# Gated MLP with channels on partitions: u and spatial products swapped, no transposes of the gated values

## The chip, the cores and the metric

The kernel runs on one core of a Trainium2 chip. The metric is the device time of one execution in microseconds. All inputs and the output lie in HBM in float32; the matmuls are in bfloat16.

## The reference

A sparse attention feeds a gated MLP. Shapes: batch 4, 8 heads, sequence 768, head size 64, so a token has 512 channels; the MLP widens them to 1024.

```python
scores = where(mask, q @ k.T / sqrt(64), -1e9)      # mask: band, edges and sampled blocks of 32
x = (softmax(scores) @ v), heads side by side       # 4 x 768 x 512
h = maximum(x @ w_in, 0.0)                          # 4 x 768 x 1024
u, v = h[..., :512], h[..., 512:]
v_n = (v - mean(v, -1)) / sqrt(var(v, -1) + 1e-6)
v_s = einsum('ts,bsd->btd', w_spatial, v_n) + b_spatial[None, :, None]
out = (u * v_s) @ w_out                             # 4 x 768 x 512
```

So the spatial product mixes tokens, its bias belongs to a token and is the same for all channels, and the output product mixes channels.

## The kernel before

The attention works on pairs of heads, 16 in all. A slot is one step of the main loop: a piece of the scores of one head (L408 for the first batch, L421 after it), the exponentials of it on ScalarE (L413, L424), and the product with the values of an earlier piece (L451, L469). VectorE divides by the row sums (L433, L434: rc, xn). Pairs after the first four get k and q transposed by a DMA (tr_dma, L367: nat to tt) and copied into kq by VectorE (split, L210: kq<-tt), five and three slots before their scores start. xn is transposed into xt, with channels on partitions and tokens along the row, by TensorE or by a DMA (L510, L501).

The MLP of a batch is dealt into the slots of the next one. Its 768 tokens are six chunks of 128; chunk c holds the tokens 6p + c. All its steps stand in a queue: for each of the six chunks a v product and a u product of NDM = 4 matmuls, then six spatial products of NCH = 6, then six output products of NDH = 4. A step is one matmul of 512 columns; run_queue takes some from the queue in each slot, about 2.25 on average, at a pace set by the number of steps left. What a step records is written out by hand in this order; each engine executes its own instructions strictly in the order recorded, and so does SP with its DMA requests. The MLP of the last batch has no slots left, and its steps run one behind another (the tail): last_x, then last_steps, then rest_steps.

Each product writes one PSUM bank (moe_ps: two banks in turn, six in the tail) and its last step records the eviction:

- v (L583, L184): relu into vn, chunk by chunk with tokens on partitions, then statistics (L588, L589) on VectorE; GpSimd makes the reciprocal deviation rstd for a group of chunks (L592, L594), and vn_one normalises a chunk in place (L184) at the earliest VN_AGE = 9 steps after its group; what is left is normalised ahead of the first spatial step.
- u: relu into un, on VectorE for batch 0 (L184), on ScalarE for the others (L617).
- spatial: one VectorE instruction adds the bias of the token (b_col, one value per partition and chunk) and multiplies by un in place (L623). Then a DMA on SP transposes two chunks of the gated values (un) into gt, with channels on partitions (L635). In the tail the sixth chunk is transposed by TensorE (g_transpose) and copied by VectorE.
- output: lhsT is gt, rhs w_out; the copy osb goes out by a DMA on SP, the very last half on ScalarE's queue (L661).

The spatial weights are loaded (ws_load), cast on GpSimd (ws_cast, L528) and transposed by DMA into w_spt in three pieces (ws_tr, L531). b_col is loaded by SP behind the first loads (L322). The order of SP's requests around slot 46 to 52 is: the transposition of pair 6 (tt), then the loads of k, q and v of a later pair, then the last piece of w_spt.

In the last batch the sequence of products is

```python
seq = m.in_steps("v0 v1 u0 v2 v3 v4 v5 u1 u2 u3 u4 u5", 3)
```

The first three steps of its first three products are recorded ahead of the transposition of the last xt, and their fourth steps behind it. xt of the last pair is copied in two parts, chunks 0 and 1 and chunks 2 to 5.

Of the kernel before, what the change touches and what calls it, by code (L numbers as in the profile page):

```python
# [10 lines left out]
FP32 = mybir.dt.float32  # L11
BF16 = mybir.dt.bfloat16
I32 = mybir.dt.int32
AF = mybir.ActivationFunctionType
ALU = mybir.AluOpType
# [11 lines left out]
def kernel(  # L27
# [16 lines left out]
    nc = tc.nc  # L44

    B, H, S, D = q.shape
# [3 lines left out]
    NCH = S // 128  # L50
# [25 lines left out]
    w_in_t = const.tile([128, NDM, DFF], BF16)  # L76
    w_out_t = const.tile([128, NDH, DM], BF16)
    w_spt = const.tile([128, NCH, NCH, 128], BF16)
    b_col = const.tile([128, NCH], FP32)
    mhalf = const.tile([128, NCH], FP32)  # L80

    kq = const.tile([128, H, 2 * S], BF16, name="kq")
# [99 lines left out]
    def ts(out, in0, s1, o0, s2=None, o1=None):  # L182
        kw = {} if o1 is None else {"op1": o1}
        nc.vector.tensor_scalar(out=out, in0=in0, scalar1=s1, scalar2=s2, op0=o0, **kw)  # L184
# [24 lines left out]
    def dve_copy(o, i):  # L209
        nc.vector.tensor_copy(out=o, in_=i)  # L210
# [47 lines left out]
    def bank(nm="ps", tag=None):  # L258
        return psum.tile([128, 1024], BF16, tag=tag or moe_tag(), bufs=2 if tag else 1, name=nm)

    def tr(ps, c, in_):
        nc.tensor.transpose(out=ps[:, c * 128:(c + 1) * 128], in_=in_, identity=ident)  # L262
# [53 lines left out]
    for i, x in enumerate(ORDER):  # L316
# [2 lines left out]
            rows(slice(2, 4), qcols(1), PL)  # L319
        for y in ORDER[i + AHEAD:i + AHEAD + 1]:  # L320
            ahead(y)
    nc.sync.dma_start(out=b_col, in_=moe_b_spatial.rearrange("(p c) -> p c", c=NCH))  # L322

    def second():
        ps2 = bank("ps2", "av")
# [191 lines left out]
    def ws_load(i):  # L517
        ws["f", i] = work.tile([128, S], FP32, tag="ws_f", bufs=6, name="ws_f")
        nc.sync.dma_start(out=ws["f", i],
                          in_=moe_w_spatial.rearrange("(p c) s -> c p s", c=NCH)[i])  # L520

    def ws_cast(i):
        if i % 2 == 0:
            ws["b", i // 2] = work.tile([128, 2, NCH, 128], BF16, tag="ws_b", bufs=2, name="ws_b")
        src = ws.pop(("f", i)).rearrange("p (s c) -> p c s", c=NCH)
        for c0 in range(0, NCH, NCH // 3):
            cs = slice(c0, c0 + NCH // 3)
            nc.gpsimd.tensor_copy(out=ws["b", i // 2][:, i % 2, cs], in_=src[:, cs])  # L528
# [9 lines left out]
    def moe_ps(last):  # L538
        if not last:
            return psum.tile([128, 512], FP32, tag=moe_tag(), bufs=1, name="ps_moe")  # L540
        tail_tags.rotate(1)
        if tail_tags[0] == "sc":
            return psum.tile([128, 1024], FP32, tag="sc", bufs=2, name="ps_sc")[:, 0:512]
        if tail_tags[0] == "moe":
            return psum.tile([128, 512], FP32, tag=moe_tag(), bufs=1, name="ps_t")
        return psum.tile([128, 512], FP32, tag="av", bufs=2, name="ps_t")

    def product(n, lhs, rhs, last, done, w=512):
        ref = {}
        out = []  # L550
        for i in range(n):
            def run(i=i):
                if i == 0:
                    ref["ps"] = moe_ps(last)
                nc.tensor.matmul(out=ref["ps"][:, 0:w], lhsT=lhs(i), rhs=rhs(i),  # L555
                                 start=(i == 0), stop=(i == n - 1))
                if i == n - 1:
                    done(ref["ps"][:, 0:w])
            out.append(run)
        return out  # L560
# [4 lines left out]
    class Moe:  # L565
        def __init__(self, b):
            self.b, self.last = b, b == B - 1
            w = lambda nm: work.tile([128, NCH, DH], BF16, tag=nm, bufs=1, name=nm)
            self.un, self.vn = w("un"), w("vn")
            self.gt = work.tile([128, NCH, NDH, 128], BF16, tag="gt", bufs=1, name="gt")  # L570
            self.mv = work.tile([128, NCH, 2], FP32, tag="mv", bufs=2)
            self.std = work.tile([128, NCH], FP32, tag="std", bufs=2)
            self.rstd = work.tile([128, NCH], FP32, tag="rstd", bufs=2)
            self.vn_due = deque()
            self.steps = 0
# [33 lines left out]
                ts(self.vn[:, tcc, :], self.vn[:, tcc, :], self.mv[:, tcc, 0:1], ALU.subtract,  # L609
                   self.rstd[:, tcc:tcc + 1], ALU.mult)  # L610

        def u_product(self, tcc):
            def done(ps):
                if self.b == 0 and tcc in U_DVE:
                    ts(self.un[:, tcc, :], ps, 0.0, ALU.max)
                else:
                    nc.scalar.activation(out=self.un[:, tcc, :], in_=ps, func=AF.Relu)  # L617
            return product(NDM, lambda g: self.xt(g, tcc), lambda g: w_in_t[:, g, 0:DH],
                           self.last, done)

        def s_product(self, tcc):
            def done(ps):
                nc.vector.scalar_tensor_tensor(out=self.un[:, tcc, :], in0=ps,  # L623
                                               scalar=b_col[:, tcc:tcc + 1],
                                               in1=self.un[:, tcc, :], op0=ALU.add,
                                               op1=ALU.mult)
                if self.last and tcc == NCH - 1:
                    return
                if self.last and tcc == NCH - 2:
                    g0 = tcc  # L630
                elif tcc % 2 == 1:
                    g0 = tcc - 1
                else:
                    return
                nc.sync.dma_start_transpose(  # L635
                    out=self.gt[:, g0:tcc + 1].rearrange("p t c n -> p (t c) n"),
                    in_=self.un[:, g0:tcc + 1, :].rearrange("p t d -> p (t d)"))
            return product(NCH, lambda s: w_spt[:, tcc, s, :], lambda s: self.vn[:, s, :],
                           self.last, done)


        def g_transpose(self):
            ps = bank("ps_g", "av")
            for d in range(NDH):
                tr(ps, d, self.un[:, NCH - 1, d * 128:(d + 1) * 128])
            dve_copy(self.gt[:, NCH - 1].rearrange("p c n -> p (c n)"), ps[:, 0:NDH * 128])

        def o_product(self, tcc, n):
            steps = []
            osb = {}  # L650
            parts = 2 if self.last and n == NCH - 1 else 1
            w = DM // parts
            for i in range(parts):
                cs = slice(i * w, (i + 1) * w)

                def done(ps, i=i, cs=cs):
                    if i == 0:
                        osb["t"] = work.tile([128, DM], FP32, tag="osb", bufs=6, name="osb")
                    on_act = self.b > 0 and (n + i) % 2 == 0
                    (act_copy if on_act else dve_copy)(osb["t"][:, cs], ps)  # L660
                    (nc.scalar if i else nc.sync).dma_start(  # L661
                        out=out[self.b].rearrange("(p c) d -> c p d", c=NCH)[tcc][:, cs],
                        in_=osb["t"][:, cs])
                steps += product(NDH, lambda d: self.gt[:, tcc, d, :],
                                 lambda d, cs=cs: w_out_t[:, d, cs], self.last, done, w)
            return steps

# [6 lines left out]
        def rest_steps(self):  # L674
            out = []
            for tcc in range(NCH):
                out += self.s_product(tcc)
            first = out[0]
            out[0] = lambda: ([self.vn_one(True) for _ in range(NCH)], first())
            for n, tcc in enumerate((0, 1, 5, 2, 3, 4) if self.last else range(NCH)):  # L680
                out += self.o_product(tcc, n)
                if self.last and n == 1:
                    out.insert(len(out) - 3, self.g_transpose)
            return out

    queue = deque()
# [20 lines left out]
    def when(slot, *fns):  # L707
        at.setdefault(slot, []).extend(fns)

    def c(f, *a, **kw):  # L710
        return lambda: f(*a, **kw)
# [57 lines left out]
    def last_x():  # L769
        moe_begin(B - 1)  # L770
        m = moe[B - 1]
        while queue:
            queue.popleft()()
        seq = m.in_steps("v0 v1 u0 v2 v3 v4 v5 u1 u2 u3 u4 u5", 3)
        n = NG - 1
        for i in (0, 1):
            for f in seq[i * NG:i * NG + n]:
                f()
        ps, xn = bank(), xn_ref.pop(("p", NP - 1))
        moe_tags.rotate(1)  # L780
        for cc in range(NCH):
            tr(ps, cc, pair_of(xn, cc))
        xt = xt_tile(NP - 1)
        for cs in (slice(0, TW), slice(TW, S)):
            dve_copy(xt[:, cs], ps[:, cs])
        for f in seq[2 * NG:2 * NG + n]:
            f()
        for i in (0, 1, 2):
            seq[i * NG + n]()
        last_steps.extend(seq[3 * NG:])  # L790
# [24 lines left out]
        when(ca, c(ws_cast, i))  # L815
    for i, sl in enumerate((24, 30, 50)):
        when(sl, c(ws_tr, i))
    when(50, *[c(w_out_load, g) for g in range(NDH)])
    when(58, *[c(w_out_cast, g, PL) for g in range(NDH)])

# [59 lines left out]
```

## Time and profile before

| what | value |
|---|---|
| median of 3 runs | 210.97 us (210.81 to 211.08) |
| the profiled execution: time, span of its instructions | 211.73 us, 209.9 us |
| TensorE busy | 201.3 us (96%) |
| weight loads busy (beside the matmuls) | 129.1 us (61%) |
| VectorE busy | 136.4 us (65%) |
| ScalarE busy | 168.8 us (80%) |
| GpSimd busy | 83.3 us (40%) |
| granted TensorE clock, mean | 0.996 |
| spatial eviction L623, 128x512 | 0.75 us each, 24 of them |
| last matmul starts, tail's spatial products start | 206.0 us, 192.9 us |

An engine's busy time is the union of its instructions. PE is TensorE's matmuls, PEld its weight loads, DVE is VectorE, ACT ScalarE, POOL GpSimd, SPq the queue of SP's requests. A timeline line gives the start, the time from the first start to the last end, engine, line and operation, out<-in, shapes and count; in brackets the idle time before it and who ended it. Matmuls overlap: the recorded time of one is longer than the distance to the next, so the pace is read from starts.

### The profile page before, as it was taken

Reading aid. Unit: us, or ns where it says so; the run is one execution under the profiler, and the core shown is the slowest. Engines: PE = TensorE matmul, PEld = TensorE weight load, DVE = VectorE, ACT = ScalarE, POOL = GpSimd, SP = SyncE. Lnnn points to the kernel's source line nnn. Section 1 sums busy time; section 2 is a strip of 40 time slices with the busy share of each in tenths; the row PEclk is TensorE's granted clock in tenths of the full one; section 3 lists DMA queues with packets and bytes.
Section 4 is the critical chain, followed back from the end, with each engine's and each line's share of the span. In section 5 each row is a group of like instructions: output and inputs, shape, how many; then the busy total and the mean of one; then the engine's idle time right before and its main releaser. Section 6 shows DMA issues by size and latency. Waiting matters only on the chain.

```text
span 209.9 us, 5319 instructions
## 1 busy us (share of the span) xinstructions
PE 201.3 (96%) x2106; PEld 129.1 (61%) x2140; DVE 136.4 (65%) x301; ACT 168.8 (80%) x222; POOL 83.3 (40%) x184
## 2 busy tenths in 40 slices
PE   8789999999999999999999999999999999999993
PEld 6569878766666666665566556665566556544441
DVE  7768987999874756484975454284985443476551
ACT  6979999999999999979998888979889787266021
POOL 6689869957828726006159051006220000012000
PEclk9999999999999999999999999999999999999998
DMA  5999799999999999999965497478501225610256
GB/s 162 330 357 344 222 314 285 251 301 359 250 338 188 264 165 296 270 219 345 210 216 112 116 247 179 153 177 262 102 3 35 53 53 116 222 54 0 50 146 228
DMA packets 64684, 41.96 MB, mean 200 GB/s; under 512 B 45716, under 2 KB 59412, under 8 KB 64660
## 3 DMA queue, kind: packets, MB, share of 16 engines
q1 hardware_dynamic: 64228, 41.24, 76.0%
q10 hardware_dynamic: 432, 0.39, 0.6%
q8 instruction: 16, 0.26, 0.5%
q14 instruction: 8, 0.07, 0.1%
HBM read 24.38 MB, written 6.29 MB: 146 GB/s over the span
## 4 chain that ended last, share of the span: by engine, by line
PE 87%; DMA 4%; DVE 2%; SPq 1%; ACT 1%; issue 1%; POOL 0%; ACTq 0%
PE ps_moe L555 31%; PE ps L421 22%; PE ps_av L469 13%; PE ps_t L555 7%; PE ps L408 6%; PE ps_av L451 4%; DMA st_k<-in_k_dram 4%; PE ps_sc L555 3%; PE ps L262 1%; SPq L108 1%; DVE kq L210 1%; ACT a_all L413 1%; DMA out_dram<-osb 1%; PE ps_av L262 1%; ACT osb L213 0%
## 5 line engine op out<-in xcount | busy, mean ns | idle before, releaser
L424 ACT ACTIVATE a_all<-ps 128x768 bf16<-128x768 f32 x144 | 113.7, 811 | 15.5 <-PE ps L421 7.2
L421 PE MATMUL ps<-kq 128*128 128x512 bf16 (+1 forms) x288 | 70.3, 325 | 0.2
L469 PEld LDWEIGHTS <-a_all 128*128 128x128 bf16 x864 | 46.6, 98 | 19.4
L469 PE MATMUL ps_av<-vv,a_all 128*128 128x65 bf16 x864 | 51.0, 194 | 0.1
L421 PEld LDWEIGHTS <-kq 128*128 128x128 bf16 x288 | 27.8, 97 | 30.1 <-issue 0.2
L555 PE MATMUL ps_moe<-w_in_t,xt 128*128 128x512 bf16 x128 | 39.4, 378 | 0.5
L413 ACT ACTIVATE a_all<-ps 128x1024 bf16<-128x1024 f32 x35 | 33.9, 1024 | 1.9 <-PE ps L408 1.4
L136 POOL CAST nat<-st_k 128x256 bf16<-128x256 f32 (+3 forms) x37 | 16.7, 482 | 42.9 <-DMA st_k<-in_k_dram 31.4
L555 PE MATMUL ps_moe<-vn,w_spt 128*128 128x512 bf16 x98 | 30.5, 378 | 0.6
L592 POOL TENSOR_SCALAR std<-mv 128x3 f32<-128x3 f32 (+1 forms) x9 | 2.1, 238 | 50.8 <-DVE mv L589 36.9
L408 PE MATMUL ps<-kq 88*128 88x256 bf16 (+1 forms) x136 | 21.0, 275 | 1.0 <-DVE kq L210 0.6
L623 DVE SCALAR_TENSOR_TENSOR un<-ps_moe,b_col,un 128x512 bf16<-128x512 f32 x18 | 13.5, 748 | 12.9 <-PE ps_moe L555 10.9
L555 PE MATMUL ps_moe<-w_out_t,gt 128*128 128x512 bf16 x66 | 20.2, 378 | 0.1
L555 PEld LDWEIGHTS <-xt 128*128 128x128 bf16 x192 | 15.2, 97 | 7.1 <-DVE xt L210 0.2
L433 DVE RECIPROCAL rc<-ps_av 128x6 f32<-128x6 f32 (+1 forms) x36 | 6.6, 184 | 19.9 <-PE ps_av L469 18.8
L434 DVE TENSOR_TENSOR xn<-ps_av,rc 128x384 bf16<-128x384 f32 (+1 forms) x36 | 18.5, 513 | 1.2
L136 POOL CAST nat<-st_q 128x256 bf16<-128x256 f32 (+2 forms) x41 | 17.2, 447 | 3.9 <-DMA st_q<-in_q_dram 3.6
L136 POOL CAST vv<-st_v 128x256 bf16<-128x256 f32 (+1 forms) x36 | 17.4, 516 | 3.1 <-DMA st_v<-in_v_dram 3.0
L588 DVE BATCH_NORM_STATS2 stats<-vn 128x6 f32<-128x512 bf16 x24 | 16.5, 688 | 1.5 <-ACT vn L583 0.9
L184 DVE TENSOR_SCALAR vn<-ps_moe 128x512 bf16<-128x512 f32 x18 | 12.3, 683 | 6.0 <-PE ps_moe L555 6.0
L451 PE MATMUL ps_av<-vv,a_all 128*128 128x65 bf16 x288 | 14.6, 194 | 1.0 <-POOL vv L136 1.0
L451 PEld LDWEIGHTS <-a_all 128*128 128x128 bf16 x288 | 13.5, 98 | 2.7 <-issue 1.5
(92 smaller groups left out, 215.5 us busy)
## 6 DMA issues: line engine op xcount, KB each, us to landing
st_v<-in_v_dram SPq DMA_DIRECT2D x16, 384.0 KB, 6.0
out_dram<-osb SPq DMA_DIRECT2D x23, 256.0 KB, 2.4
st_k<-in_k_dram SPq DMA_DIRECT2D x15, 384.0 KB, 4.4
st_q<-in_q_dram SPq DMA_DIRECT2D x12, 384.0 KB, 4.9
ws_f<-in_moe_w_spatial_dram SPq DMA_DIRECT2D x6, 384.0 KB, 4.7
w_f<-in_moe_w_in_dram SPq DMA_DIRECT2D x8, 256.0 KB, 5.6
w_f<-in_moe_w_out_dram SPq DMA_DIRECT2D x4, 256.0 KB, 5.6
st_q<-in_q_dram SPq DMA_DIRECT2D x3, 256.0 KB, 6.9
```

Source lines behind the costliest of these rows:

```text
L136: eng.tensor_copy(out=dst, in_=src)
L184: nc.vector.tensor_scalar(out=out, in0=in0, scalar1=s1, scalar2=s2, op0=o0, **kw)
L408: nc.tensor.matmul(out=ps[:, at:at + n * TW], lhsT=kq[0:KR, h, ci * 128:(ci + 1) * 128], rhs=kq[0:KR, h, qcols(t0, n)], start=True, stop=True)
L413: nc.scalar.activation(out=out, in_=ps, func=AF.Exp, scale=0.125)
L421: nc.tensor.matmul(out=ps[:, n0:n1], lhsT=kq[:, j % H, ci * 128:(ci + 1) * 128], rhs=kq[:, j % H, S + n0:S + n1], start=True, stop=True)
L424: nc.scalar.activation(out=a_ref["h", j][:, ci, :], in_=ps[:, 0:S], func=AF.Exp, scale=0.125)
L434: nc.vector.tensor_tensor(out=out, in0=ps[:, :, 0:D], in1=rc[:, 0:n].to_broadcast([128, n, D]), op=ALU.mult)
L451: nc.tensor.matmul(out=av_ref[u][:, to, :], lhsT=a_ref[u][:, at:at + 128], rhs=vv[pp % NVV][:, h, ci, :], start=(ci == 0), stop=(ci == NCH ...
L469: nc.tensor.matmul(out=av_ref[j][:, qc, :], lhsT=a_ref["h", j][:, ci, qc * 128:(qc + 1) * 128], rhs=vv[p % NVV][:, h, ci, :], start=(ci == ...
L555: nc.tensor.matmul(out=ref["ps"][:, 0:w], lhsT=lhs(i), rhs=rhs(i), start=(i == 0), stop=(i == n - 1))
L588: nc.vector.bn_stats(out=stats, in_=self.vn[:, tcc, :])
L623: nc.vector.scalar_tensor_tensor(out=self.un[:, tcc, :], in0=ps, scalar=b_col[:, tcc:tcc + 1], in1=self.un[:, tcc, :], op0=ALU.add, op1=AL ...
```

## The change

The u product takes w_in as the stationary operand and xt as the moving one, so u comes out with channels on partitions and tokens along the row. The spatial product takes the normalised v as the stationary operand and w_spt as the moving one, with the same result layout. un then has the layout that the output product needs, gt and its transposes go, and the output product reads un.

An area of a product is nd blocks of 128 channels by n chunks of 128 tokens, with nd x n = 4, so that it fills a bank and a step still streams 512 columns: one matmul of 512 where nd is 1, two of 256 where nd is 2. For u, batch 0 has six areas of two blocks by two chunks; the others two of these and four of one block by chunks 2 to 5. The spatial products have four areas of one block by chunks 0 to 3 and two of two blocks by chunks 4 and 5.

The bias now lies along the row and is the same on all partitions: SP loads the 768 values to all 128 partitions (b_load, slot 46), and VectorE copies them into the order of the chunks (b_row, slot 52). The eviction is two VectorE instructions: the add of b_row from PSUM into sb (float32), and the product with un in place.

In the last batch v2 is moved ahead of u0 and the output chunks come in the order 0 to 5.

```diff
-    b_col = const.tile([128, NCH], FP32)
+    b_row = const.tile([128, S], FP32)
...
-    nc.sync.dma_start(out=b_col, in_=moe_b_spatial.rearrange("(p c) -> p c", c=NCH))
...
+    def b_load():
+        ws["b_nat"] = work.tile([128, S], FP32, tag="ws_f", bufs=6, name="b_nat")
+        nc.sync.dma_start(out=ws["b_nat"], in_=moe_b_spatial.partition_broadcast(128))
...
-            self.un, self.vn = w("un"), w("vn")
-            self.gt = work.tile([128, NCH, NDH, 128], BF16, tag="gt", bufs=1, name="gt")
+            self.vn = w("vn")
+            self.un = work.tile([128, NDH, S], BF16, tag="un", bufs=1, name="un")
...
+        def in_place(self, d0, nd, c0, n):
+            return self.un[:, d0:d0 + nd, c0 * 128:(c0 + n) * 128]
+
+        def by_columns(self, k, d0, nd, c0, n, lhs, rhs, done):
+            ref, out = {}, []
+            mms = [(x, i) for x in range(nd) for i in range(k)]
+
+            def run(j):
+                if j == 0:
+                    ref["ps"] = moe_ps(self.last)
+                for x, i in mms[j * nd:(j + 1) * nd]:
+                    o = ref["ps"][:, x * n * 128:(x + 1) * n * 128]
+                    nc.tensor.matmul(out=o.rearrange("p (c t) -> p c t", c=n),
+                                     lhsT=lhs(i)[:, (d0 + x) * 128:(d0 + x + 1) * 128],
+                                     rhs=rhs(i), start=(i == 0), stop=(i == k - 1))
+                if j == k - 1:
+                    done(ref["ps"][:, 0:512].rearrange("p (d t) -> p d t", d=nd))
+            return [lambda j=j: run(j) for j in range(k)]
+
+        def u_product(self, i):
+            if self.b == 0:
+                area = (2 * (i % 2), 2, TC * (i // 2), TC)
+            else:
+                area = (2 * i, 2, 0, 2) if i < 2 else (i - 2, 1, 2, NCH - 2)
+            d0, nd, c0, n = area
...
-        def s_product(self, tcc):
+            return self.by_columns(
+                NDM, *area, lambda g: w_in_t[:, g, 0:DH],
+                lambda g: xt_ref[self.b * NG + g][:, c0 * 128:(c0 + n) * 128].rearrange(
+                    "p (c t) -> p c t", c=n), done)
+
+        def s_product(self, i):
+            area = (i, 1, 0, NCH - 2) if i < NDH else (2 * (i - NDH), 2, NCH - 2, 2)
+            d0, nd, c0, n = area
+
             def done(ps):
-                nc.vector.scalar_tensor_tensor(out=self.un[:, tcc, :], in0=ps,
-                                               scalar=b_col[:, tcc:tcc + 1],
-                                               in1=self.un[:, tcc, :], op0=ALU.add,
-                                               op1=ALU.mult)
...
-                nc.sync.dma_start_transpose(
-                    out=self.gt[:, g0:tcc + 1].rearrange("p t c n -> p (t c) n"),
-                    in_=self.un[:, g0:tcc + 1, :].rearrange("p t d -> p (t d)"))
-            return product(NCH, lambda s: w_spt[:, tcc, s, :], lambda s: self.vn[:, s, :],
-                           self.last, done)
-
-
-        def g_transpose(self):
-            ps = bank("ps_g", "av")
...
+                sb = work.tile([128, 512], FP32, tag="sb", bufs=2, name="sb").rearrange(
+                    "p (d t) -> p d t", d=nd)
+                nc.vector.tensor_tensor(
+                    out=sb, in0=ps, op=ALU.add,
+                    in1=b_row[:, None, c0 * 128:(c0 + n) * 128].to_broadcast([128, nd, n * 128]))
+                nc.vector.tensor_tensor(out=self.in_place(*area), in0=sb,
+                                        in1=self.in_place(*area), op=ALU.mult)
+            return self.by_columns(NCH, *area, lambda s: self.vn[:, s, :],
+                                   lambda s: w_spt[:, c0:c0 + n, s, :], done)
...
-                steps += product(NDH, lambda d: self.gt[:, tcc, d, :],
+                steps += product(NDH, lambda d: self.un[:, d, tcc * 128:(tcc + 1) * 128],
                                  lambda d, cs=cs: w_out_t[:, d, cs], self.last, done, w)
...
-            for n, tcc in enumerate((0, 1, 5, 2, 3, 4) if self.last else range(NCH)):
-                out += self.o_product(tcc, n)
-                if self.last and n == 1:
-                    out.insert(len(out) - 3, self.g_transpose)
+            for n in range(NCH):
+                out += self.o_product(n, n)
...
-        seq = m.in_steps("v0 v1 u0 v2 v3 v4 v5 u1 u2 u3 u4 u5", 3)
+        seq = m.in_steps("v0 v1 v2 u0 v3 v4 v5 u1 u2 u3 u4 u5", 3)
...
+    when(46, b_load)
+    when(52, lambda: nc.vector.tensor_copy(out=b_row.rearrange("d (c p) -> d c p", c=NCH),
+                                           in_=ws.pop("b_nat").rearrange("d (p c) -> d c p", c=NCH)))
```

More of the change, by code (lines that the diff above doesn't have):

```diff
@@ L610, in vn_one @@
                    self.rstd[:, tcc:tcc + 1], ALU.mult)
-        def u_product(self, tcc):
+        def in_place(self, d0, nd, c0, n):
[14 more added lines that the diff above has]
+            return [lambda j=j: run(j) for j in range(k)]
@@ L613, in done @@
+        def u_product(self, i):
[4 more added lines that the diff above has]
+            d0, nd, c0, n = area
             def done(ps):
-                if self.b == 0 and tcc in U_DVE:
-                    ts(self.un[:, tcc, :], ps, 0.0, ALU.max)
-                else:
-                    nc.scalar.activation(out=self.un[:, tcc, :], in_=ps, func=AF.Relu)
@@ L618, in u_product @@
-            return product(NDM, lambda g: self.xt(g, tcc), lambda g: w_in_t[:, g, 0:DH],
-                           self.last, done)
-        def s_product(self, tcc):
-            def done(ps):
-                nc.vector.scalar_tensor_tensor(out=self.un[:, tcc, :], in0=ps,
-                                               scalar=b_col[:, tcc:tcc + 1],
-                                               in1=self.un[:, tcc, :], op0=ALU.add,
-                                               op1=ALU.mult)
[L627 to L634, printed above, removed]
-                nc.sync.dma_start_transpose(
-                    out=self.gt[:, g0:tcc + 1].rearrange("p t c n -> p (t c) n"),
-                    in_=self.un[:, g0:tcc + 1, :].rearrange("p t d -> p (t d)"))
-            return product(NCH, lambda s: w_spt[:, tcc, s, :], lambda s: self.vn[:, s, :],
-                           self.last, done)
@@ L642, in g_transpose @@
-        def g_transpose(self):
-            ps = bank("ps_g", "av")
-            for d in range(NDH):
-                tr(ps, d, self.un[:, NCH - 1, d * 128:(d + 1) * 128])
-            dve_copy(self.gt[:, NCH - 1].rearrange("p c n -> p (c n)"), ps[:, 0:NDH * 128])
+                if self.b == 0 and i in U_DVE:
+                    ts(self.in_place(*area), ps, 0.0, ALU.max)
+                else:
+                    nc.scalar.activation(out=self.in_place(*area), in_=ps, func=AF.Relu)
+            return self.by_columns(
+                NDM, *area, lambda g: w_in_t[:, g, 0:DH],
+                lambda g: xt_ref[self.b * NG + g][:, c0 * 128:(c0 + n) * 128].rearrange(
+                    "p (c t) -> p c t", c=n), done)
```

## The prediction

> **What bounds the kernel now.** I read the page's busy times, then the busy time by stretch, then who waited for whom on TensorE, and last the timeline around the two places where the change lengthens VectorE's work. Busy times, then TensorE, its weight loads, VectorE, ScalarE and GpSimd in two stretches:
>
> ```profile
> PE 201.3 (96%) x2106; PEld 129.1 (61%) x2140; DVE 136.4 (65%) x301; ACT 168.8 (80%) x222; POOL 83.3 (40%) x184
> ...
> 44.00:180.00 136.00, 134.61 (x1411) 83.35 (x1434) 84.23 (x171) 118.86 (x159) 47.05 (x112) 1.00 0.79 191
> 180.00:206.00 26.00, 25.84 (x141) 12.39 (x141) 15.83 (x34) 9.11 (x16) 2.29 (x4) 1.00 0.34 101
> ```
>
> From 44 us on TensorE is busy 99% of the time at full granted clock (1.00). That it also streams is seen from starts: eight 512-column matmuls take 1.89 us, which is seven steps of 0.216 and one of 0.378, and the qk, av and product matmuls follow each other without room. The single holes of 0.05 us, one in 5 us, are lost records (192 weight loads from xt stand beside 175 matmuls). So time is won only by less TensorE work, and every new wait of TensorE after 44 us is added to the end in full. VectorE (62% in the first stretch) costs nothing until TensorE waits for it. The first place is the first spatial product of batch 0, which needs all six chunks of normalised v:
>
> ```profile
> 54.46 1.38 DVE L184 TENSOR_SCALAR un<-ps_moe 128x512 bf16<-128x512 f32 x2
> 55.47 0.38 PE L555 MATMUL ps_moe<-vn,w_spt 128*128 128x512 bf16 x1
> 55.76 0.89 DVE L184 TENSOR_SCALAR vn<-vn,mv,rstd 128x512 bf16<-128x512 bf16 x2
> 56.20 0.59 PE L555 MATMUL ps_moe<-vn,w_spt 128*128 128x512 bf16 x2
> 57.15 0.38 PE L555 MATMUL ps_moe<-vn,w_spt 128*128 128x512 bf16 x1
> 57.88 0.59 PE L555 MATMUL ps_moe<-vn,w_spt 128*128 128x512 bf16 x2
> ...
> 47.74 4.16 SPq L367 DMA_TRANSPOSE tt<-nat  x1
> 51.95 0.64 SPq L108 DMA_DIRECT2D st_k<-in_k_dram  x1
> ```
>
> Chunks 4 and 5 are ready at 56.65, and the product's steps 4 and 5 start at 57.88 and 58.10: 1.4 us of cover. The new bias request stands on SP between the two lines at the bottom. The second place is the same step of the last batch:
>
> ```profile
> 188.45 0.88 POOL L594 TENSOR_TENSOR rstd<-std,mhalf 128x3 f32<-128x3 f32 x1
> 188.65 0.18 DVE L589 BATCH_NORM_AGGREGATE mv<-stats 128x2 f32<-128x6 f32 x1
> 188.75 0.66 DVE L588 BATCH_NORM_STATS2 stats<-vn 128x6 f32<-128x512 bf16 x1
> ...
> 189.55 0.70 DVE L184 TENSOR_SCALAR vn<-vn,mv,rstd 128x512 bf16<-128x512 bf16 x2
> 190.17 0.69 DVE L588 BATCH_NORM_STATS2 stats<-vn 128x6 f32<-128x512 bf16 x1
> 190.89 0.18 DVE L589 BATCH_NORM_AGGREGATE mv<-stats 128x2 f32<-128x6 f32 x1
> 190.99 0.38 DVE L184 TENSOR_SCALAR vn<-vn,mv,rstd 128x512 bf16<-128x512 bf16 x1
> ...
> 192.46 1.06 DVE L184 TENSOR_SCALAR vn<-vn,mv,rstd 128x512 bf16<-128x512 bf16 x3 [1.09 <-POOL rstd L594]
> 192.91 2.75 PE L555 MATMUL ps_t<-vn,w_spt 128*128 128x512 bf16 x12
> ```
>
> Here chunk 5 is ready at 193.52 and its step starts at 192.91 + 5 x 0.216 = 193.99: 0.47 us of cover.
>
> **The change, part by part.** *TensorE work.* Every product streams as many columns as before, but the two-block areas do it with pairs of 256: 24 more matmuls for u in batch 0, 8 in each later batch, 12 per batch for the spatial products, 24 + 24 + 48 = 96. Four 256-column matmuls take 0.60 us with a last one of 0.272, so 0.109 each; a pair is 0.218 against 0.216. With rounding 0.2 to 0.35 us, taken as **+0.3**. The weight loads stay covered: 0.109 is the pace of qk matmuls that each have their own.
>
> *Transposes.* The twelve gt requests leave SP (1.23 us each) and the DMA queues. TensorE waits for none of them, so they give nothing; SP's other requests come earlier, and TensorE waits for no load either. In the tail four identity matmuls go (0.056 each) and a wait of 0.04: **-0.26**.
>
> *Add and product.* One instruction of 0.75 becomes two. The add reads PSUM like the xn row (0.557 for 384, 0.424 for 256), so 0.69 for 512; the product reads fp32 and bf16 from SBUF, not shown, bounded by 0.44 (vn from vn) and 0.75 (the row it replaces), taken as 0.69 because it has two inputs like the xn row. 24 x (1.38 - 0.75) = 15 us more on VectorE, on the path only where somebody waits. The bank is freed after 0.69 instead of 0.75. In the tail TensorE makes a product in 1.29, VectorE now needs 1.4: with a first start 1.56 after the phase begins, the fourth product ends at 1.56 + 4 x 1.4 = 7.2, and the output products load it at 7.74 + 3 x 0.216 = 8.4; the sixth ends at 10.0 and is loaded at 11.6. Covered, with 1.2 us to spare. In the middle, two spatial products (5 us of slots) bring 1.3 us more to a VectorE that idles 0.5 to 1.6 us before each; the next kq copies have a margin of about 2 us before their qk. Nothing. If that cover went, each product would add up to 0.1.
>
> [...]
>
> *The bias.* b_col's request at 22.4 goes. A row of 3 KB is read 128 times (393 KB) behind the transposing request that SP ends at 51.91. By the trace's landing marks that one lands at 56.57 and the three loads of 384 KB behind it at 57.62, 58.65 and 59.67: in order, 1.03 apart. So the row lands at 57.6 and the loads 1.03 later, which GpSimd's casts, 4 us idle before w_out, can take. On VectorE a new copy into b_row stands behind the two un evictions, ahead of chunks 4 and 5. VectorE is there at 55.84 and stands until 57.65. The copy: 3,072 bytes a partition within SBUF, as kq<-tt moves in 0.556 (0.852 beside GpSimd's work); the other bound is fp32 at the PSUM pace, 0.95; I take 0.65, nearer to the row with the same bytes. Then the two vn in 0.89: ready at 59.2, loaded at 59.25 instead of 58.10. Behind the waiting copy are queued chunks 4 and 5, the normalising of the attention output and two kq copies; the latter have their 2 us and TensorE is late itself. **+1.2**, from 0 (landing by 56.5) to 1.75 (copy 0.95, vn 0.6 each).
>
> [...]
>
> *The tail's order.* v2 now goes ahead of u0, so its statistics are recorded earlier and the recorder, which lets chunks 0 and 1 follow nine steps later, places their normalising ahead of the statistics of chunk 4, not behind them. VectorE ends chunk 3's statistics at 188.83, but rstd is there only at 189.33: idle for 0.54. Then vn 0 and 1 from 189.37, statistics 4 from 189.99, vn 2 from 190.81, statistics 5 from 191.12 instead of 190.17: 0.95 late. GpSimd's rstd and the last three vn follow by the same: chunk 5 is ready at 194.47, not 193.52. Being the stationary operand now, it must be there before its load. 0.95 - 0.47 + 0.1 = **+0.6**; from 0.2 (if vn 2 costs nothing there) to 0.75.
>
> Sum: 0.3 - 0.26 + 1.2 + 0.6 = +1.84. The profiled execution took 211.73 with a span of 209.9; it would become 213.6 with 211.8. The median of the runs is 0.76 below the profiled one, so 210.97 + 1.84 = **212.8 us**.
>
> **The rivals.** *The bias is in time (the side where nothing measurable changes).* Between 53.5 and 55.0 the queue moved almost nothing (window 44 to 62 in 40 slices):
>
> ```profile
> DMA  9999999399899999999999208999999999999969
> ```
>
> Without that pause in the transposing transfer the row lands at 56.1, before the deciding 56.5, and the wait of 1.2 goes. Left is 0.04 plus the tail's 0.2 to 0.6: 211.2 to 211.6; below a tail of 0.38 that is no measurable change. For it: SP and the queue lose b_col's 768 tiny elements before; against it: SP reaches the request only when GpSimd lets the transposition go. Chance 0.17.
>
> *The broadcast is slow.* All 128 reads go to the same 3 KB; no row shows that. If it takes as long as the slowest transposing transfer (3.4 behind the one before), it lands 2.4 later, and TensorE waits 3.6: 215 (213.8 to 216). Against: 24-byte pieces of b_col took 0.2. Chance 0.13.
>
> *VectorE becomes the bound* in batch 0's spatial phase, where GpSimd works too: a product of 1.1 instead of 0.69 beside the lateness of 2 us from the bias uses up the kq margin, another 0.5 to 2: 213.5 to 214.8. Chance 0.07.
>
> *Holes in TensorE's records are waits* that a bank freed 0.06 earlier shortens: 12 x 0.06, which only with both new waits absent makes 210.3. The count of loads speaks against it. Chance 0.03.
>
> **How the numbers follow.** The forecast with both waits (212.2 to 213.4) gets the remaining 0.60. About 0.2% (0.42 us) is what a measurement of this kernel can tell from no change. Faster: 0.03. Within: half of the first rival, 0.09. Slower: 0.88. The range 211.3 to 214.6 leaves out the lower part of the first rival, half of the second and the last.
>
> **What would show it.** The b_row copy waiting some 1.8 us for its transfer at about 56; TensorE waiting for vn there about 1.2 and at 193 to 194 about 0.6; no wait for un; spatial pairs of about 1.4 on VectorE; 256-column starts 0.109 apart. The prediction is wrong if TensorE has no wait for vn, or waits for un or kq.

## The result and the profile after

The changed kernel takes 213.61 us (median of 15 runs, 211.6 to 216.25) beside 211.1 us for the kernel before (15 runs, 210.51 to 211.9). The ratio is 1.0083, 95% interval 1.0059 to 1.0107: slower by 0.8%, or 1.75 us. Ratio and interval leave out runs more than 1.5% above the fastest of their kernel, here five of the changed kernel at 215.1 to 216.3, in which it cost most; with them the medians are 2.51 us apart.

The profiled execution took 211.90 us with a span of 210.1, one of the fastest of its kernel. The busy times, the two stretches, and TensorE's longest waits (line waited for: us in total, times, longest), all of the changed kernel:

```profile
PE 204.5 (97%) x2232; PEld 139.2 (66%) x2232; DVE 153.0 (73%) x325; ACT 168.9 (80%) x222; POOL 87.6 (42%) x184
...
44.00:180.00 136.00, 135.99 (x1494) 89.34 (x1492) 96.71 (x187) 118.35 (x159) 50.67 (x111) 1.00 0.70 173
180.00:206.00 26.00, 25.92 (x157) 14.09 (x156) 18.72 (x38) 9.00 (x16) 2.23 (x4) 1.00 0.20 74
...
PEld L627 <- DVE vn L184: 1.3, 4, 0.6
PEld L407 <- DVE kq L210: 1.0, 2, 0.8
```

VectorE has 16.6 us more to do (153.0 against 136.4), and from 44 to 180 us it is busy 71% of the time instead of 62%. Transfers have become fewer. Neither decides: the new line among the waits is the first of the last two, normalised v ahead of a spatial product. It falls in two places, those of the two groups of rows shown before. VectorE and SP around the first:

```profile
47.13 3.98 SPq L366 DMA_TRANSPOSE tt<-nat  x1
51.15 0.58 SPq L523 DMA_DIRECT2D b_nat<-in_moe_b_spatial_dram  x1
...
53.91 1.35 DVE L184 TENSOR_SCALAR un<-ps_moe 128x512 bf16<-128x512 f32 x2
55.87 1.08 DVE L835 COPY b_row<-b_nat 128x768 f32<-128x768 f32 x1 [0.61 <-DMA b_nat<-in_moe_b_spatial_dram]
56.88 0.90 DVE L184 TENSOR_SCALAR vn<-vn,mv,rstd 128x512 bf16<-128x512 bf16 x2
...
59.89 0.68 DVE L658 TENSOR_TENSOR sb<-ps_moe,b_row 128x512 f32<-128x512 f32 x1
60.60 0.69 DVE L661 TENSOR_TENSOR un<-sb,un 128x512 bf16<-128x512 f32 x1
```

The copy stands 0.61 us for its row, and chunks 4 and 5 of vn are normalised only at 56.88 to 57.78; TensorE's load of chunk 5, for the sixth step, follows at 57.83 (this weight load is marked with 0.30 of idle time, and the matmuls come 0.3 us late in all). VectorE and the waiting weight loads around the second place:

```profile
189.23 0.74 DVE L184 TENSOR_SCALAR vn<-vn,mv,rstd 128x512 bf16<-128x512 bf16 x2 [0.53 <-POOL rstd L597]
189.88 0.69 DVE L591 BATCH_NORM_STATS2 stats<-vn 128x6 f32<-128x512 bf16 x1
190.60 0.18 DVE L592 BATCH_NORM_AGGREGATE mv<-stats 128x2 f32<-128x6 f32 x1
190.70 0.38 DVE L184 TENSOR_SCALAR vn<-vn,mv,rstd 128x512 bf16<-128x512 bf16 x1
191.00 0.69 DVE L591 BATCH_NORM_STATS2 stats<-vn 128x6 f32<-128x512 bf16 x1
...
193.23 1.06 DVE L184 TENSOR_SCALAR vn<-vn,mv,rstd 128x512 bf16<-128x512 bf16 x3 [1.32 <-POOL rstd L597]
194.77 0.69 DVE L658 TENSOR_TENSOR sb<-ps_t,b_row 128x512 f32<-128x512 f32 x1 [0.48 <-PE ps_t L627]
195.56 0.69 DVE L661 TENSOR_TENSOR un<-sb,un 128x512 bf16<-128x512 f32 x1
...
193.69 0.10 PEld L627 LDWEIGHTS <-vn 128*128 128x128 bf16 x1 [0.57 <-DVE vn L184]
194.02 0.10 PEld L627 LDWEIGHTS <-vn 128*128 128x128 bf16 x1 [0.23 <-DVE vn L184]
194.34 1.62 PEld L627 LDWEIGHTS <-vn 128*128 128x128 bf16 x9 [0.23 <-DVE vn L184]
```

The statistics of the last chunk come at 191.00 instead of 190.17, and the last three vn at 193.23 instead of 192.46. Three weight loads wait, once for each of chunks 3, 4 and 5. What that delays is read from the matmul starts, since an idle weight loader is not yet an idle TensorE: 0.25 + 0.11 + 0.11 = 0.47 us.

The two spans differ by only 0.2 us, less than these waits. Ahead of 38 us, in code that the change hardly touches, this execution was 0.8 us in front: the 31st of ScalarE's exponential pieces starts at 34.48 instead of 35.32, and before, the first product with the values waited 1.0 us at 11.4 for vv, and here it did not. From there on the lead is given back: 0.23 by 48 us (its cause stays open), 0.34 at the bias, 0.11 in the 40 pairs of batches 1 and 2, 0.22 in the tail. All nine traces of changed kernels in this document lie 0.7 to 1.5 us in front of the kernel before at 13.6 us. Of that kernel there is one trace, and its span of 209.9 is 0.7 above the median of the 23 runs beside the first experiments; so it was probably the late one, but no second trace shows it. A difference of two spans is therefore no cost by itself.

### The profile page after: what moved, and what is told of

Its sections match the earlier page's. It is cut to its first block, busy times and chain, and to the rows that moved or that the text cites. A ratio compares the mean times of both kernels' runs of the same rounds, so it can differ in the third digit from the quotient of the medians.

```text
span 210.1 us, 5529 instructions
## 1 busy us (share of the span) xinstructions
PE 204.5 (97%) x2232; PEld 139.2 (66%) x2232; DVE 153.0 (73%) x325; ACT 168.9 (80%) x222; POOL 87.6 (42%) x184
## 4 chain that ended last, share of the span: by engine, by line
PE 90%; DVE 5%; ACT 2%; POOL 1%; issue 0%; POOLq 0%; ACTq 0%; DVEq 0%
PE ps L420 22%; PE ps_moe L627 19%; PE ps_moe L558 15%; PE ps_av L468 13%; PE ps L407 6%; PE ps_av L450 4%; PE ps_t L558 3%; PE ps_t L627 2%; PE wps L178 2%; DVE stats L591 1%; ACT a_all L412 1%; PE ps_sc L627 1%; DVE kq L210 1%; PE ps_sc L558 1%; PE ps L262 1%; DVE vn L184 1%
## 5 line engine op out<-in xcount | busy, mean ns | idle before, releaser
L468 PEld LDWEIGHTS <-a_all 128*128 128x128 bf16 x864 | 46.6, 98 | 19.4
L468 PE MATMUL ps_av<-vv,a_all 128*128 128x65 bf16 x864 | 51.0, 194 | 0.0
L136 POOL CAST nat<-st_k 128x256 bf16<-128x256 f32 (+3 forms) x37 | 18.5, 530 | 41.7 <-DMA st_k<-in_k_dram 41.5
L627 PE MATMUL ps_moe<-w_spt,vn 128*128 128x512 bf16 (+1 forms) x144 | 32.9, 325 | 0.0
L627 PE MATMUL ps_moe<-xt,w_in_t 128*128 128x256 bf16 (+1 forms) x112 | 22.8, 302 | 0.0
L558 PE MATMUL ps_moe<-w_in_t,xt 128*128 128x512 bf16 x72 | 22.3, 378 | 0.0
L558 PE MATMUL ps_moe<-w_out_t,un 128*128 128x512 bf16 x72 | 21.5, 378 | 0.0
L627 PEld LDWEIGHTS <-vn 128*128 128x128 bf16 x192 | 15.5, 97 | 5.4 <-DVE vn L184 1.3
L661 DVE TENSOR_TENSOR un<-sb,un 128x512 bf16<-128x512 f32 x24 | 17.3, 720 | 1.5
L658 DVE TENSOR_TENSOR sb<-ps_moe,b_row 128x512 f32<-128x512 f32 x18 | 12.4, 687 | 5.2 <-PE ps_moe L627 4.9
```

What stands on the lines that cost most here:

```text
L136: eng.tensor_copy(out=dst, in_=src)
L468: nc.tensor.matmul(out=av_ref[j][:, qc, :], lhsT=a_ref["h", j][:, ci, qc * 128:(qc + 1) * 128], rhs=vv[p % NVV][:, h, ci, :], start=(ci == ...
L627: nc.tensor.matmul(out=o.rearrange("p (c t) -> p c t", c=n), lhsT=lhs(i)[:, (d0 + x) * 128:(d0 + x + 1) * 128], rhs=rhs(i), start=(i == 0) ...
L661: nc.vector.tensor_tensor(out=self.in_place(*area), in0=sb, in1=self.in_place(*area), op=ALU.mult)
```

## The experiments

The theory of the prediction, A in the expectations: two waits of TensorE for vn, the first set by when the bias row lands, the second by VectorE's order in the tail, and the rest of the change cancels. Against it stand accounts by which the longer VectorE work, or the swapped layout itself, costs the time. The first four kernels ran beside 23 runs of the kernel before (median 211.3), the last four beside 23 others (211.09).

**The changed kernel again** (after_again), for a second trace of the same code.

> The changed kernel itself, for more executions and a second profile. In the first profile TensorE waited 0.3 us for the normalised v of batch 0 and 0.5 in the tail, which with the pairs gives about 1 us, while the runs lay 1.8 above the kernel before and spread by 3 us. Theory A (the bias row's landing varies, and the wait for it with it): this profile shows another wait at that place, between 0 and 3 us, and the time goes with it. Rival B (the start of the kernel varies, nothing else): the wait there is again 0.3 and the difference lies before 20 us.

Measured 214.56 us (213.11 to 216.0, 6 runs), ratio 1.0165 (1.0117 to 1.0213). The profiled execution took 215.26. Its copy, its waits, its row of granted clock over the span, and two stretches (the clock is the third number from the end):

```profile
47.42 5.22 SPq L366 DMA_TRANSPOSE tt<-nat  x1
52.69 0.58 SPq L523 DMA_DIRECT2D b_nat<-in_moe_b_spatial_dram  x1
...
58.03 0.86 DVE L835 COPY b_row<-b_nat 128x768 f32<-128x768 f32 x1 [3.48 <-DMA b_nat<-in_moe_b_spatial_dram]
...
PEld L627 <- DVE vn L184: 3.9, 5, 2.7
...
PEclk9999999999969999999999999999999999999999
...
56.00:60.00 4.00, 1.47 (x13) 0.65 (x11) 1.94 (x5) 1.43 (x2) 2.19 (x7) 0.94 1.02 289
60.00:66.00 6.00, 6.00 (x56) 3.64 (x55) 4.33 (x8) 3.81 (x5) 1.23 (x2) 0.76 1.14 262
```

The same program waits 2.7 us here where it waited 0.3. SP held the transposing request for 5.22 us instead of 3.98, so the bias request behind it left 1.5 us later and its row landed 2.2 later. And behind the wait the clock drops: a round of one product step, the scores and the values takes 1.40 us there (weight loads of vn at 60.93 and 62.33) where it took 0.74 in the first trace (58.54 and 59.28), so about half speed. From the two stretches that is 2 x (0.06 x 4 + 0.24 x 6) = 3.4 us at half speed, of which half, 1.7, is lost. The profiled execution has a mean clock of 0.991 (1 - 0.5 x 3.4 / 213.5 is 0.992), and so have the five slowest of the 15 runs above, at 0.991 or 0.992, the others at 0.996 to 1.0. Of the six runs here the three slowest have that lower clock.

**The bias requested earlier** (bias_early): the row is there long before its copy.

```diff
-    when(46, b_load)
+    when(34, b_load)
```

> The bias row is requested at slot 34 instead of 46, so it lies there when VectorE comes to the copy. Theory A: the wait for the row and TensorE's wait at the first spatial product of batch 0 go or fall under 0.2 us, the time falls by 0.5 to 1.5 us to 211.4 to 212.3, and the spread falls to that of the kernel before (1.4 us). Rival B or C (the vector engine's load as a whole holds TensorE): time and spread stay.

Measured 211.56 us (210.76 to 213.94, 12 runs), ratio 1.0009 (0.9988 to 1.003). The spread is that of the 23 runs of the kernel before beside it (210.25 to 213.44), not the 1.4 us that was expected. The copy is at 55.19 without a wait and takes 1.10; of the waits for vn the tail's three are left. So the bias request was worth 1.0083 - 1.0009 = 0.0074, or 1.56 us, most of the loss; the two intervals do not overlap. By the medians of all runs it was worth more, 2.51 - 0.26 = 2.25 us.

**The copy behind chunks 4 and 5** (copy_late), the request where it was.

```diff
-    when(52, lambda: nc.vector.tensor_copy(out=b_row...
+    when(53, lambda: nc.vector.tensor_copy(out=b_row...
```

> The bias request stays, but the copy into b_row is recorded one slot later, behind the normalising of the last two chunks of v. Theory A: TensorE no longer waits for v in batch 0, and the time falls as with the early request, 211.4 to 212.3; what waits behind the copy now (the attention's normalising, two kq copies) has 2 us of cover. Rival D (the 393 KB themselves in the queue cost the time): no gain here and none with the early request.

Measured 211.46 us (211.14 to 213.91, 12 runs), ratio 1.0032 (0.9999 to 1.0066). VectorE still waits longer than in the first trace, but behind the two vn:

```profile
54.96 0.94 DVE L184 TENSOR_SCALAR vn<-vn,mv,rstd 128x512 bf16<-128x512 bf16 x2
57.59 1.01 DVE L835 COPY b_row<-b_nat 128x768 f32<-128x768 f32 x1 [1.68 <-DMA b_nat<-in_moe_b_spatial_dram]
```

TensorE does not wait for vn in batch 0, and for kq only 0.04 us at the matmuls. So it is not the late row that costs, but what is queued behind its copy on VectorE.

**The old order in the tail** (tail_order): chunks 0 to 2 of the last batch are normalised behind the statistics of chunk 4 again.

```diff
-                        self.vn_due.extend((t, self.steps + VN_AGE + VN_STEP * i)
+                        self.vn_due.extend((t, self.steps + VN_AGE + (4 if self.last and grp == 3 and t < 3 else 0) + VN_STEP * i)
```

> Only the last batch: the normalising of chunks 0 to 2 is recorded four steps later, so that VectorE again makes the statistics of chunks 4 and 5 ahead of what they had ahead of them before. Theory A: TensorE's wait of 0.46 us at 193 to 194 goes, the time falls by 0.4 to 0.6. Rival (v as the stationary operand is what waits): a wait of 0.2 or more stays there.

Measured 213.29 us (6 runs), ratio 1.0105 (1.0065 to 1.0145): by the times nothing can be told, because the bias wait varies by more than this. The trace can: the weight loads of the normalised v run on without a wait,

```profile
193.19 2.69 PEld L627 LDWEIGHTS <-vn 128*128 128x128 bf16 x13
```

and the tail from its first spatial matmul to its last matmul takes 206.29 - 193.41 = 12.88 us, against 206.15 - 192.80 = 13.35 in the changed kernel and 206.04 - 192.91 = 13.13 before. The order cost 0.47, and without it the tail is 0.25 shorter than before: the identity transposes. With v still the stationary operand no wait is left, so the rival falls. The bias wait of this execution is 0.7 at the matmuls, with the row at 56.46.

**Both mended** (early_order): the edits of bias_early and tail_order.

> The early bias request and the tail's order together. Theory A (the two waits for v are the whole loss): no wait for vn is left, only the 96 pairs (+0.26) against the transposes of the tail (-0.26): 0.2 to 0.5 us under the early request alone, the same as the kernel before within 0.3 us, 210.8 to 211.3. Rival C (VectorE's 15 us more hold TensorE somewhere): 0.5 or more above it.

Measured 210.96 us (210.23 to 213.06, 12 runs), ratio 0.9996 (0.9967 to 1.0024). No weight load waits for vn anywhere, the tail is 12.88 us, the span 209.0. With both waits gone the new layout takes the same time as the old one, within 0.3% (0.7 us) either way; that it beats it is not shown.

**The bias requested later** (bias_later), behind the loads of k, q and v: the dose in the other direction.

```diff
-    when(46, b_load)
+    when(49, b_load)
```

> The bias request at slot 49, behind the loads of k, q and v, so that it lands about 3 us later, at 59 to 61. Theory A: VectorE waits 3 us longer, TensorE waits 3 to 6 us for v in batch 0, and the granted clock falls to half for a stretch of 3.4 us behind that wait, as in the second profile, which costs 1.7 more: 216 to 219 us. Rival B (the start, or chance, makes the spread and the clock): 213 to 214.5 as the changed kernel.

Measured 217.83 us (217.15 to 218.0, 4 runs), ratio 1.0322 (1.0289 to 1.0354).

```profile
59.92 0.85 DVE L835 COPY b_row<-b_nat 128x768 f32<-128x768 f32 x1 [5.25 <-DMA b_nat<-in_moe_b_spatial_dram]
...
PEld L627 <- DVE vn L184: 5.7, 5, 4.4
...
PEclk9999999999979999999999999999999999999999
```

As A expected: the row lands 1.9 us later than in after_again and TensorE waits 1.7 longer, again with 3.4 us at half clock behind it (from 60 to 66 us the mean clock is 0.72, and 2 x 0.28 x 6 = 3.4). So the loss follows the landing.

**One operation instead of two** (one_op): add and product in one instruction, with the constant 1.0 in place of the bias; no load, no copy.

```diff
-                nc.vector.tensor_tensor(
-                    out=sb, in0=ps, op=ALU.add,
-                    in1=b_row[:, None, c0 * 128:(c0 + n) * 128].to_broadcast([128, nd, n * 128]))
-                nc.vector.tensor_tensor(out=self.in_place(*area), in0=sb,
-                                        in1=self.in_place(*area), op=ALU.mult)
+                nc.vector.scalar_tensor_tensor(out=self.in_place(*area), in0=ps, scalar=1.0,
+                                               in1=self.in_place(*area), op0=ALU.add,
+                                               op1=ALU.mult)
...
-    when(46, b_load)
-    when(52, lambda: nc.vector.tensor_copy(out=b_row...
```

> Leaves out the bias row: the eviction is one instruction with the constant 1.0 in place of the bias; no load of the row, no copy. All else as in the changed kernel, the tail's order too. Theory A: the same time as the early request (211.3 to 211.9, ratio 1.000 to 1.003), since add and product apart are hidden. Rival C: 0.5 to 1.5 us less than the early request.

Measured 211.67 us (211.28 to 213.78, 12 runs), ratio 1.0032 (1.0006 to 1.0058), no better than bias_early with its two operations (1.0009). In the tail a single operation of 0.69 comes every 1.3 us, at TensorE's pace. The second instruction is hidden: the account by VectorE's work falls with this run, the one by the layout with early_order.

**No copy at all** (no_copy_order): the add reads the row as it was loaded, every sixth value; request at slot 46, tail order mended.

```diff
+                bias = b_nat.rearrange("d (p c) -> d c p", c=NCH)[:, c0:c0 + n]
...
-                    out=sb, in0=ps, op=ALU.add,
-                    in1=b_row[:, None, c0 * 128:(c0 + n) * 128].to_broadcast([128, nd, n * 128]))
+                    out=sb.rearrange("p d (c t) -> p d c t", c=n), op=ALU.add,
+                    in0=ps.rearrange("p d (c t) -> p d c t", c=n),
+                    in1=bias[:, None].to_broadcast([128, nd, n, 128]))
...
-    when(52, lambda: nc.vector.tensor_copy(out=b_row...
```

> The bias request stays at slot 46, but there is no copy into b_row: the add reads the row in the order of its loading, every sixth value. The tail's order is the mended one. Theory A: the first add comes at 59 to 60 us, behind the landing at 56 to 58, so nothing waits: 210.8 to 211.3 like the early request with the mended order. If the stride makes the add slower (0.75 to 1.4 instead of 0.69), the tail gets the difference: up to 0.7 more.

Measured 212.85 us (6 runs), ratio 1.0105 (1.0063 to 1.0148). VectorE in the tail, TensorE's new wait, and SP's output requests; the last line is SP in early_order, for comparison:

```profile
201.02 1.05 DVE L658 TENSOR_TENSOR sb<-ps_t,b_nat 128x512 f32<-128x512 f32 x1
202.11 0.69 DVE L662 TENSOR_TENSOR un<-sb,un 128x512 bf16<-128x512 f32 x1
202.72 1.06 DVE L658 TENSOR_TENSOR sb<-ps_sc,b_nat 128x512 f32<-128x512 f32 x1
203.81 0.69 DVE L662 TENSOR_TENSOR un<-sb,un 128x512 bf16<-128x512 f32 x1
204.42 1.28 DVE L210 COPY osb<-ps_t 128x512 f32<-128x512 f32 x2
...
PEld L557 <- DVE un L662: 1.1, 2, 0.6
...
202.26 5.32 SPq L680 DMA_DIRECT2D out_dram<-osb  x6
```
```profile
201.72 4.29 SPq L679 DMA_DIRECT2D out_dram<-osb  x6
```

The strided add takes 1.06 instead of 0.69, a pair 1.77 instead of 1.40, and TensorE makes a product in 1.29. Six pairs are now too slow: TensorE waits twice for un (0.44 us at the matmuls), and VectorE comes to its osb copies late, so SP's six requests end at 207.58 instead of 206.01. The span is 2.0 longer than that of early_order, more than was expected: 0.26 ahead of the tail, 0.44 of waits, the rest behind the last matmul. This is the rival of a VectorE that becomes the bound, made real by 0.37 us per product.

## Why the prediction was right, point by point

The forecast of +1.84 us (+0.87%) stands beside +1.75 (+0.83%, 1.25 to 2.26), and beside +2.51 between the medians of all 15 runs. The two places and what happens in them came as forecast. That the number is this close is in part luck: its largest term, the bias, was one number where single executions gave 0.3 to 4.4 us. By its terms:

| term | forecast | measured |
|---|---|---|
| 96 more pairs of 256 columns | +0.3 | 40 pairs cost 0.11, so +0.26 |
| identity transposes of the tail | -0.26 | -0.25 |
| twelve gt requests gone | 0 | not seen apart; early_order equals before within 0.7 |
| add and product apart | 0 | 0 (one_op) |
| bias | +1.2 (0 to 1.75) | 0.3, 0.7 and 4.4 in three traces; 1.56 over the runs (2.25 by all medians) |
| tail's order | +0.6 (0.2 to 0.75) | +0.47 |

*Add and product.* Both take 0.69 as taken (medians of 0.692 for the add from PSUM and 0.693 for the product; single products of batch 0 up to 0.86), a pair in the tail 1.40 as worked out, and nobody waits for un. VectorE has 16.6 us more to do. The two instructions cost time only once the cover is used up, as no_copy_order shows: six pairs of 1.40, against a product of 1.29 on TensorE, stay within it, and six of 1.77 do not.

*The bias.* The mechanism was right: a row behind the transposing request, a copy that waits for it, and two vn behind the copy. In the first trace the copy waited 0.61 where 1.8 was forecast, and TensorE 0.3 where 1.2 was. Three sizes were off, in both directions. First, the copy takes 1.08 where 0.65 was taken and 0.95 was the upper bound. It takes 0.85 where GpSimd casts nothing beside it, 0.86 where a cast runs 0.17 us into it, and 1.01 to 1.15 in the five traces where a cast is still running for 0.30 to 0.40 us after its start. And a cast that starts during the copy ends 0.27 to 0.28 us behind the copy's end and takes 1.04 to 1.06 instead of 0.40 (four traces). So beside each other both take longer: the cast by 0.64 to 0.66 us, the copy by 0.16 to 0.30, which is 0.1 to 0.15 less than what is left of the cast. The row with the same bytes was the wrong neighbour: it reads its bytes in order, this copy reads every sixth float32, and in no_copy_order such reading made the add take 1.06 instead of 0.69. Second, the row does not land 1.03 behind the transfer ahead, like a plain load of 384 KB, but 1.33 in the first trace and 2.15 in after_again, and behind plain loads 0.97 (bias_later) to 2.35 (bias_early). Third, the deciding landing was not 56.5 but about 55.5: by the longer copy (0.43) and by a TensorE that was ahead there.

*What was missed* is the spread. The landing was taken as one number, from one execution; with the request at slot 46 it was five numbers in five:

| | SP ends the transposing request | row lands | TensorE's matmuls late by |
|---|---|---|---|
| changed kernel | 51.11 | 55.84 | 0.3 |
| tail_order | 51.42 | 56.46 | 0.7 |
| copy_late | 52.03 | 57.56 | 0 (copy behind vn) |
| no_copy_order | 52.32 | 57.37 | 0 (no copy) |
| after_again | 52.64 | 58.01 | 2.7, and 1.7 by the clock |

The rival "in time" is thus nearly the first row, and the rival "slow broadcast" nearly the last: they were not two ways the change could go, but two ends of what one program does. The times of the 15 runs, 211.6 to 216.25, spread over both; that it is the landing that spreads them is shown by five traces and by the clock of the five slowest, not by a trace of each. The 15 of the kernel before beside them lie within 1.4 us. The pause in the queue on which the first rival rested did not go away; it moved with the transposing transfer:

```profile
DMA  9999999989999999920399989999999978991008
```

In this window of the changed kernel (44 to 62 us in 40 slices) it ends at 53.0 and the transposing transfer lands at 54.5; before it ended at 55.0 and the transfer landed at 56.6.

*The tail's order.* The idle time ahead of vn 0 (0.53), the later statistics and the later rstd came as written. The last three vn started 0.77 later on the timeline, 0.88 later against the tail's first spatial matmul, where 0.95 was forecast, and the matmuls lost 0.47. Less the 0.47 of cover, the lateness alone would cost 0.41; about 0.06 is left for the earlier need at the weight load, where 0.1 was taken.

*The holes* in TensorE's records, the last rival, are no waits: the changed kernel has as many loads as matmuls (2232 each), is busy 135.99 of 136.00 us in the first stretch, and did not become faster by it.

## What to carry to other kernels

Swapping the operands of a product saved its transposes, but they were off the path, and it made the late operand the stationary one: ask of every input whether it is now needed at the weight load (three loads of vn waited 0.57, 0.23 and 0.23 us in the tail), and what is queued on its producer ahead of it. A small constant, loaded just in time, held up what was recorded behind its first use (with the request at slot 46 the copy waited 0.61 to 3.48 us for its row); request it early or put its use behind the work that others wait for, since here either mended it (bias_early, copy_late). Where a transfer stands behind a request whose duration varies (3.98 to 5.84 us here), forecast the time as a range over executions, and compare medians of many runs, not two profiles.

## What was unexpected in the hardware

- A wait of TensorE of 2.7 us, and one of 4.4, were each followed by 3.4 us at about half the granted clock (mean of 0.76 and 0.72 from 60 to 66 us); waits of 0.7 and less at the same place were not. The wait thus cost 1.7 us more than itself. Two of the four runs of bias_later have a mean clock of 0.984, which by the same sum would be 6.9 us at half speed, an estimate; no trace shows these.
- Reading every sixth float32 made an add of 512 take 1.06 us instead of 0.69.
- SP held one and the same transposing request for 3.98 to 5.84 us in ten traces, around the same place. The traces put SP's wait there down to GpSimd's cast of ws_b (4.1 us in the kernel before, 4.7 in the changed one), but that cast ended 0.08 us ahead of the end of SP's request in the first and 0.77 us ahead in the second. What sets the duration was not tried, and it stays open; the landing of the bias row hangs on it.
